# A gated mix of linear and local attention on one core: first loads in another order, and the range-test branch ahead of the last outputs

## The chip, the cores and the metric

The kernel runs on one core of one Trainium2 chip. The metric is the device time of one execution in microseconds. Three runs of the kernel before took 500.43, 500.95 and 501.45 us; the median is 500.95 us.

## What is computed

Two attention blocks A and B read the same tokens `x` (2048 tokens of 1024 features, bf16); a sigmoid gate per token mixes their outputs. Cut to what matters:

```python
x = A_x
g = sigmoid((x * gate_w).sum(-1, keepdims=True))
# A: linear attention, 32 heads of 32
q, k, v = split(x @ A_wqkv)
phi = lambda t: where(t > 0, t + 1, exp(t)) + 1e-6
kv, z = einsum("bhsd,bhse->bhde", phi(k), v), einsum("bhsd->bhd", phi(k))
o = einsum("bhqd,bhde->bhqe", phi(q), kv) / (einsum("bhqd,bhd->bhq", phi(q), z)[..., None] + 1e-6)
a = merge_heads(o) @ A_wo
# B: each token attends to 8 tokens, 2 apart, at and before its own
q, k, v = split(x @ B_wqkv)
attn = softmax(where(idx >= 0, q . k[idx] * scale, -1e9))    # idx = s - 2 * (0..7)
b = merge_heads(attn . v[idx]) @ B_wo
return g * a + (1 - g) * b
```

## The kernel before

**A program written as a list, ordered by a planner.** The function `plan` lists operations with `P.op` (engine, instruction, estimated cost, what is read and written, a priority). `Prog.schedule` (L120) plays the list through with those estimates, taking on each engine the ready operation of lowest priority number, and so fixes each engine's order. `move` (L1337) leaves it to the planner whether ScalarE (ACT) or VectorE (DVE) empties a PSUM bank. The planner makes six passes and keeps the shortest plan. `Prog.emit` (L202) then writes each engine's stream: the waits of an operation, the operation, its semaphore. Nothing is decided at run time but one branch, told of below. So an engine that waits holds up all that stands behind it in its stream, DMA issues included; SP's stream is nearly nothing but DMA issues.

**Stages on TensorE (PE).** First nine matmuls on zeros (L1348). Then B's values: 16 tiles of 128 tokens by two halves of 512 columns, each a group of eight 128x128x512 matmuls (L1309), copied from PSUM to `vst` (eight buffers, L1340 on DVE, L1341 on ACT) and stored to `vB_hbm` by SP (L1376). Then B's keys and queries by 512 tokens, with local attention of finished tokens (L1416, L1435, L1442) fitted between; A's keys, values and their sums (L1517); the fold of those sums into `A_wo` (L1569); A's queries, denominators (L1596) and outputs; last, B's output projection for each token tile (`final`, L1634 to 1656): eight matmuls into each of two banks, one DVE operation that mixes a bank with A's part into the output buffer `o` (two buffers, L1649), and one DMA of the tile by SP (L1655). The last tile is done in three parts of 512, 256 and 256 columns, each with a DMA of its own.

**The first loads.** Matmuls want `x` with features on partitions, so `xT` is loaded with transposing DMAs from SP. The first 512 tokens come as four transposes of 256 features each (L1297), the other tiles as one transpose for each 128 tokens (`load_x`, L1285). ScalarE issues the first half of B's value weight in four quarters (L1296), and, after a wait for a matmul, its second half in two loads (L1365). TensorE runs the first four tiles together, quarter by quarter (L1360 to 1364). The tiles go in the order 0 to 7 with the first weight half, 0 to 7 with the second, then 8 to 11 and 12 to 15 in the same way (L1353). Tiles 8 to 15, `gate_w` and the loads of `xn` (the tokens once more, for the gate, L1387) may not be issued before tile 5's first group (`x_op`, L1372). `early` (L1351) names the groups after which later weights are loaded.

**The range test.** Parts of the fast path hold only for inputs in some range. Maxima are collected on the way; after the third output tile of `final` a last chain of small DVE operations makes one number, `flag` (L1696), 1 for inputs in range. `tail` (L1718) ends each engine's stream: wait for `flag`, load it into a register (L1721); on SP, wait for every DMA semaphore of the program (39 of them, L1723); then a branch (L1725), in whose arm, for flag 0, stands a general path for any input (`progs`, hundreds of instructions on an engine). With these inputs the flag is 1 and the branch jumps over that arm.

Of the kernel before, what the change touches and what calls it, by code (L numbers as in the profile page):

```python
# [13 lines left out]
D = 1024  # L14
# [6 lines left out]
SCALE = DH ** -0.5  # L21
SZ = {BF16: 2, F32: 4, I32: 4}
# [39 lines left out]
class Prog:  # L62
# [139 lines left out]
    def emit(self, block, tail):  # L202
# [35 lines left out]
        def run(e, eng):  # L238
            for o, waits in plan[eng]:
                for s, v in waits:  # L240
                    e.wait_ge(s, v)
                ins = o.fn(e)
                ins.then_inc(o.val[0], 16 if o.chan is not None else 1)
            tail(e, eng)

        self.final = [(self.csem[c], n) for c, n in chan_n.items()]
        self.counts = cnt
# [855 lines left out]
def build_kernel(nc, A_x, A_wqkv, A_wo, B_x, B_wqkv, B_wo, gate_w, out):  # L1103
# [117 lines left out]
    def plan(seen):  # L1221
# [63 lines left out]
        def load_x(t, prio, after=()):  # L1285
            e_, r = t // 8, t % 8
            return P.op("sp", lambda e: e.dma_start_transpose(xT[:, :, t * 128:(t + 1) * 128], x2[e_, r * 128:(r + 1) * 128, :]),  # L1287
                        1.5, writes=[xT.part((0, 8), (t * 128, (t + 1) * 128))], prio=prio, chan="x%d" % t, lat=1.15, after=after)

        def load_w(slot, half, src, c0, prio, d0=0, d1=8, eng="sp", after=()):  # L1290
            n = d1 - d0
            return P.op(eng, lambda e: e.dma_start(ws[slot][:, d0:d1, half * 512:half * 512 + 512], src[:, d0:d1, c0:c0 + 512]), 0.4 + 0.2 * n,
                        writes=[ws[slot].part((d0, d1), (half * 512, half * 512 + 512))], prio=prio, chan="w%d_%d_%d" % (slot, half, d0), lat=0.42 * n, after=after)

        for d in range(0, 8, 2):
            load_w(0, 0, Bw, 2048, 0.1 + 0.1 * d, d, d + 2, "act")  # L1296
            P.op("sp", lambda e, d=d: e.dma_start_transpose(xT[:, d:d + 2, 0:512], x2[0, 0:512, 128 * d:128 * d + 256]),  # L1297
                 1.3, writes=[xT.part((d, d + 2), (0, 512))], prio=d / 2, chan="xd%d" % d, lat=1.2)
        for t in range(4, 8):
            load_x(t, 4 + t)  # L1300
# [50 lines left out]
        early = {(1, 1): (1, 0, Bw, 1024, 21), (4, 1): (2, 0, Bw, 0, 22), (7, 1): (1, 1, Bw, 1536, 23), (10, 1): (2, 1, Bw, 512, 24),  # L1351
                 (12, 1): (3, 0, Aw, 1024, 25), (14, 1): (3, 1, Aw, 1536, 26)}
        for t, half in [(t, half) for t0, n in ((0, 8), (8, 4), (12, 4)) for half in range(2) for t in range(t0, t0 + n)]:  # L1353
            vt, vs = vst.next()
            xs, xr = x_tile(t)
            w, wr = w_half(0, half)
            if t < 4 and half == 0:
                if t == 0:
                    first = [main.next() for _ in range(4)]
                    for d in range(0, 8, 2):  # L1360
                        for t_ in range(4):
                            if d == 6 and t_ == 0:
                                o_w = o
                            o = group(first[t_], x_tile(t_)[0], w, [xT.part((d, d + 2), (t_ * 128, t_ * 128 + 128)), ws[0].part((d, d + 2), (0, 512))], d, d + 2)
                    for d in range(0, 8, 4):  # L1365
                        load_w(0, 1, Bw, 2560, 3 + 0.1 * d, d, d + 4, "act", after=[o_w])
                bank = first[t]
            else:
                bank = main.next()
                o = group(bank, xs, w, [xr, ws[0].part((0, 8), (half * 512, half * 512 + 512))])  # L1370
                if (t, half) == (5, 0):
                    x_op = o  # L1372
                    for t_ in range(8, NT):
                        load_x(t_, 4 + t_, [o])
# [5 lines left out]
        P.op("sp", lambda e: e.dma_start(gwb[:, :], gate_w[None, :].to_broadcast([128, D])), 0.6, writes=[gwb.all()], prio=29, chan="gw", lat=0.8, after=[x_op])  # L1380
# [4 lines left out]
        for t in range(NT):  # L1385
            xt, xs_ = xn.next()
            P.op("sp", lambda e, t=t, xt=xt: e.dma_start(xt[:, :], x2[t // 8, (t % 8) * 128:(t % 8) * 128 + 128, :]), 0.6, writes=[xt.all()], chan="xn%d" % xs_, lat=1.0, after=[x_op])  # L1387
# [246 lines left out]
        def final(t):  # L1634
# [4 lines left out]
            for f0, f1 in parts:  # L1639
# [13 lines left out]
                if t == NT - 1 or f1 == 1024:  # L1653
                    c = f0 if t == NT - 1 else 0
                    P.op("sp", lambda e, e_=e_, r=r, o_=o_, c=c, f1=f1: e.dma_start(out2[e_, r * 128:(r + 1) * 128, c:f1], o_[:, c:f1]), 0.5,  # L1655
                         reads=[o_.part((c, f1))], chan="out%d_%d" % (os_, c), lat=1.0)
# [61 lines left out]
    def tail(e, eng):  # L1718
        reg = e.alloc_register("fast_ok")
        e.wait_ge(*flag_op.val)  # L1720
        e.reg_load(reg, flag[0:1, 0:1])  # L1721
        if eng == "sp":
            for s, v in P.final:  # L1723
                e.wait_ge(s, v)
        with e.If_eq(reg, 0):  # L1725
            for s, v in P.final + [(P.esem[x], n) for x, n in P.counts.items() if n]:
                e.wait_ge(s, v)
            for th in progs[eng]:
                th(e)

    with nc.Block() as block:
        P.emit(block, tail)
# [34 lines left out]
```

## Time and profile before

| what | value | how to read it |
|---|---|---|
| median of three runs | 500.95 us | the time that a change is measured against |
| the profiled execution | 500.95 us | its own time |
| span of that execution | 499.1 us | from its first instruction to its last |
| ACT busy | 165.8 us (33%) | one of the two engines that empty PSUM |
| L1309, values and other groups | 748 and 921 matmuls, 167.5 and 210.4 us | projections, by the order of their operands |
| L1645 | 259 matmuls, 55.3 us | B's output projection |
| DMA queue of SP (q1) | 48834 packets, 45.89 MB | nearly all transfers |
| DMA queue of ACT (q10) | 2144 packets, 2.10 MB | six weight loads at the start |

The page cuts the span into 40 slices of 12.5 us; in the row of the DMA engines a digit is the busy share of a slice in tenths, 9 for 90% and more:

```profile
PE   8899999999999999999999999999999999999995
DVE  2221336997577777556554645596865734524442
DMA  9999993331003037201100100501574315101122
```

In a line of a timeline stand the start, the length, the engine, the line of code, the operation and what it writes and reads, and in brackets how long the engine was idle before it and what ended that. A q behind an engine's name marks its sequencer, which loads registers, branches and issues DMAs.

### The profile page before, as it was taken

The page shows a single profiled execution, that of the slowest core. Times are in us where ns is not written, and L with a number is a line of the kernel's source. Part 1 is how long each engine was busy: PE and PEld are TensorE (multiplying, and loading weights), DVE is VectorE, ACT ScalarE, POOL GpSimd, SP SyncE. Part 2 cuts the span into 40 slices and gives each one's busy share as a digit, 9 for nine tenths or more (in the row PEclk, how much of TensorE's full clock was granted, in tenths as well). Part 3 has the DMA queues.
Part 4 walks back from the last instruction along what each step waited for, and adds up shares of the span by engine and source line. Part 5 has one row for each costly group of instructions (what it writes and reads, how often), then busy time and mean ns, then how long its engine had stood idle before and what let it go on. Part 6 is the DMA issues. An engine that isn't in the chain of part 4 may idle for free.

```text
span 499.1 us, 11394 instructions
## 1 busy us (share of the span) xinstructions
PE 480.8 (96%) x5055; PEld 227.4 (46%) x5121; DVE 276.7 (55%) x489; ACT 165.8 (33%) x285; POOL 5.1 (1%) x27
## 2 busy tenths in 40 slices
PE   8899999999999999999999999999999999999995
PEld 2344444444444444554554454444444444444442
DVE  2221336997577777556554645596865734524442
ACT  1111111123333445565655556355423322020000
POOL 3000000000000000000000000000000000000000
PEclk9999999999999999999999999999999999999999
DMA  9999993331003037201100100501574315101122
GB/s 193 206 204 301 324 353 104 105 107 42 2 24 106 24 80 206 56 24 41 29 22 25 35 12 4 168 2 35 159 188 101 90 24 165 62 4 66 65 84 68
DMA packets 51035, 48.80 MB, mean 98 GB/s; under 512 B 20129, under 2 KB 38945, under 8 KB 50978
## 3 DMA queue, kind: packets, MB, share of 16 engines
q1 hardware_dynamic: 48834, 45.89, 32.8%
q10 hardware_dynamic: 2144, 2.10, 1.9%
q8 instruction: 42, 0.69, 0.5%
q14 instruction: 15, 0.12, 0.1%
HBM read 34.34 MB, written 9.44 MB: 88 GB/s over the span
## 4 chain that ended last, share of the span: by engine, by line
PE 88%; DMA 4%; SPq 3%; DVE 2%; issue 2%; ACT 0%; ACTq 0%
PE ps_all L1309 70%; PE ps_all L1645 11%; PE ps_all L1416 2%; PE ps_all L1435 2%; DMA xT<-in_A_x_dram 2%; SPq L1297 2%; DMA rb<-rc_hbm 1%; PE ps_all L1517 1%; SPq L1609 1%; SPq L1287 1%; DMA rc_hbm<-ra 1%; PE ps_all L1442 1%; DVE zsel L1559 1%; DVE pq L1322 0%; PE ps_all L1596 0%
## 5 line engine op out<-in xcount | busy, mean ns | idle before, releaser
L1309 PE MATMUL ps_all<-w,xT 128*128 128x512 bf16 x921 | 210.4, 384 | 8.1 <-issue 4.3
L1309 PE MATMUL ps_all<-xT,w 128*128 128x512 bf16 x748 | 167.5, 379 | 2.3 <-issue 1.9
L1309 PEld LDWEIGHTS ps_all<-w,xT 128*128 128x128 bf16 x960 | 92.1, 99 | 114.6 <-issue 9.2
L1309 PEld LDWEIGHTS ps_all<-xT,w 128*128 128x128 bf16 x768 | 73.8, 98 | 89.1 <-issue 1.8
L1645 PE MATMUL ps_all<-w,qT 128*128 128x512 bf16 (+1 forms) x259 | 55.3, 372 | 0.3
L1645 PEld LDWEIGHTS ps_all<-w,qT 128*128 128x128 bf16 x264 | 25.9, 98 | 29.6
L1340 DVE CAST vst<-ps_all 128x512 bf16<-128x512 f32 x17 | 11.6, 691 | 48.5 <-PE ps_all L1309 48.5
L1320 DVE TENSOR_SCALAR e<-e 128x512 bf16<-128x512 bf16 x64 | 18.3, 290 | 34.4 <-ACT e L1318 17.2
L1422 ACT ACTIVATE E<-ps_all 128x1824 bf16<-128x1824 f32 (+1 forms) x18 | 30.4, 1688 | 10.2 <-PE ps_all L1416 9.5
L1318 ACT ACTIVATE e<-ps_all 128x512 bf16<-128x512 f32 x32 | 19.1, 597 | 42.8 <-PE ps_all L1309 42.3
L1425 DVE TENSOR_TENSOR E<-E,msk 128x1824 bf16<-128x1824 bf16 (+1 forms) x18 | 19.8, 1102 | 22.4 <-ACT E L1422 22.4
L1649 DVE SCALAR_TENSOR_TENSOR o<-ps_all,gm,xT 128x512 bf16<-128x512 f32 (+1 forms) x25 | 18.2, 730 | 22.9 <-PE ps_all L1645 22.8
L1316 ACT ACTIVATE e<-ps_all 128x512 bf16<-128x512 f32 x32 | 19.1, 597 | 26.6 <-PE ps_all L1309 25.8
L1341 ACT ACTIVATE vst<-ps_all 128x512 bf16<-128x512 f32 x15 | 9.0, 597 | 53.3 <-PE ps_all L1309 53.3
L1454 DVE TENSOR_TENSOR qT<-ps_all,L 128x456 bf16<-128x456 f32 (+1 forms) x36 | 21.0, 627 | 6.2 <-ACT L L1452 5.0
L1274 DVE TENSOR_TENSOR mx<-mx,kT 128x1024 bf16<-128x1024 bf16 x32 | 20.8, 688 | 3.0 <-ACT kT L1341 2.8
L1322 DVE SCALAR_TENSOR_TENSOR pk<-ps_all,e 128x512 bf16<-128x512 f32 x32 | 21.9, 688 | 0.7
L1451 ACT ACTIVATE L<-ps_all 128x456 f32<-128x456 f32 (+1 forms) x36 | 17.8, 547 | 12.4 <-PE ps_all L1435 12.4
L1274 DVE TENSOR_TENSOR mx<-mx,qT 128x1024 bf16<-128x1024 bf16 x32 | 20.7, 688 | 1.4 <-ACT qT L1344 1.2
L1341 ACT ACTIVATE kT<-ps_all 128x512 bf16<-128x512 f32 x16 | 9.6, 597 | 34.2 <-PE ps_all L1309 34.2
L1344 ACT ACTIVATE qT<-ps_all 128x512 bf16<-128x512 f32 x16 | 9.6, 597 | 33.1 <-PE ps_all L1309 33.1
L1612 DVE TENSOR_TENSOR xT<-xT,rb 128x512 bf16<-128x512 bf16 x24 | 16.3, 688 | 6.8 <-DMA rb<-rc_hbm 6.3
(72 smaller groups left out, 284.9 us busy)
## 6 DMA issues: line engine op xcount, KB each, us to landing
rb<-rc_hbm SPq DMA_DIRECT2D x32, 256.0 KB, 4.8
w<-in_A_wqkv_dram SPq DMA_DIRECT2D x6, 1024.0 KB, 7.7
v<-vB_hbm SPq DMA_DIRECT2D x36, 128.0 KB, 2.7
vB_hbm<-vst SPq DMA_DIRECT2D x32, 128.0 KB, 5.0
w<-in_B_wqkv_dram SPq DMA_DIRECT2D x4, 1024.0 KB, 6.3
xn<-in_A_x_dram SPq DMA_DIRECT2D x16, 256.0 KB, 2.6
out_dram<-o SPq DMA_DIRECT2D x15, 256.0 KB, 2.0
w<-in_A_wo_dram SPq DMA_DIRECT2D x8, 256.0 KB, 3.6
```

The source lines that it names most:

```text
L1274: P.op("dve", lambda e, m=m, op=op: e.tensor_tensor(m[:, 0:n], m[:, 0:n], src, op), 0.08 + n / 1920.0, reads=[m.all(), reg], writes=[m.all()],
L1309: last = e.matmul(bank.ap(), lhs(dc), rhs(dc), start=(dc == 0), stop=(dc == 7))
L1316: P.op("act", lambda e: e.activation(e_[:, :], bank.ap(), ACT.Exp), act(512), reads=[bank.iv], writes=[e_.all()])
L1318: P.op("act", lambda e: e.activation(e_[:, :], bank.ap(), ACT.Exp, accum_out=qe[:, col:col + 1]), act(512) + 0.1, reads=[bank.iv], writes= ...
L1320: P.op("dve", lambda e: e.tensor_scalar(e_[:, :], e_[:, :], 1.0, 1e-6, op0=ALU.min, op1=ALU.add), 0.25, reads=[e_.all()], writes=[e_.all()])
L1322: P.op("dve", lambda e: e.scalar_tensor_tensor(out=dst, in0=bank.ap(), scalar=0.0, in1=e_[:, :], op0=ALU.max, op1=ALU.add), dps(512), read ...
L1341: fa = lambda e: e.activation(dst, src(), ACT.Copy)
L1422: P.op("act", lambda e: e.activation(E[:, 0:32 * nq].rearrange("p (j q) -> p j q", j=4), ps[:, 4:8, 0:8 * nq], ACT.Exp), act(32 * nq), rea ...
L1425: P.op("dve", lambda e: e.tensor_tensor(ev(), ev(), m[:, :, :].rearrange("p r q -> p (r q)")[:, None, :].to_broadcast([128, 16, 2 * nq]), ...
L1454: P.op("dve", lambda e, L=L, h=h, q0=q0: e.tensor_tensor(qT[:, :, q0:q0 + nq], SO[h].ap(0, n).rearrange("p (c q) -> p c q", c=8), L[:, 0:n ...
L1645: last = e.matmul(bank.ap(0, f1 - f0), qT[:, dc, t * 128:(t + 1) * 128], ws[3][:, dc, f0:f1], start=(dc == 0), stop=(dc == 7))
L1649: P.op("dve", lambda e, bank=bank, o_=o_, t=t, n=n, i0=i0, i1=i1, tgt=tgt, c0=c0: e.scalar_tensor_tensor(out=o_[:, i0 * 128:i1 * 128].rear ...
```

## The change

Two parts of the program change.

At the start, the four transposes of 512 tokens go; every tile is loaded by `load_x`. The first weight half is loaded in four quarters, two from ScalarE and two from SP behind tile 0; the second half in four quarters from SP behind tile 3 (each `load_w` of two feature blocks). The tiles are worked through in blocks of four, each with the first and then the second half; tile 0's groups wait quarter by quarter. The gates on later loads go, and `early`'s first entry is moved from group (1, 1) to (2, 0). Two latency estimates of the planner are changed.

At the end, an engine's stream is cut before the operations that the planner starts in its last microseconds (`BACK`: 19 for SP, 14 for DVE, 30 for ACT, none for the others), and not before the flag. The cut-off rest is written into both arms of the branch. In the new order of instructions the arms hold seven output DMAs on SP, nine mixing operations on DVE, and the program's last output DMA, columns 768 to 1024 of the last tile, on ScalarE. In the arm for inputs in range SP waits at its end only for the semaphores of DMAs that nothing else waited for, four of them, and the arm ends with a jump of its own.

```diff
+BACK = {"sp": 19, "dve": 14, "act": 30}
...
-    def emit(self, block, tail):
+    def awaited(self, chan):
+
+        return all(o.users for o in self.ops if o.chan == chan)
+
+    def emit(self, block, tail, flag_op):
...
-        def run(e, eng):
-            for o, waits in plan[eng]:
+        def go(e, ops):
+            for o, waits in ops:
                 for s, v in waits:
                     e.wait_ge(s, v)
                 ins = o.fn(e)
                 ins.then_inc(o.val[0], 16 if o.chan is not None else 1)
-            tail(e, eng)
+
+        def run(e, eng):
+            ops = plan[eng]
+            k = len(ops)
+            while k and ops[k - 1][0].start > max(self.span - BACK.get(eng, 0), flag_op.end + 3):
+                k -= 1
+            go(e, ops[:k])
+            tail(e, eng, lambda: go(e, ops[k:]))
 
         self.final = [(self.csem[c], n) for c, n in chan_n.items()]
+        self.last = [(self.csem[c], n) for c, n in chan_n.items() if not self.awaited(c)]
...
-        def load_x(t, prio, after=()):
+        def load_x(t, prio):
...
-                        1.5, writes=[...], prio=prio, chan="x%d" % t, lat=1.15, after=after)
+                        1.5, writes=[...], prio=prio, chan="x%d" % t, lat=1.3)
...
-        for d in range(0, 8, 2):
-            load_w(0, 0, Bw, 2048, 0.1 + 0.1 * d, d, d + 2, "act")
-            P.op("sp", lambda e, d=d: e.dma_start_transpose(xT[:, d:d + 2, 0:512], x2[0, 0:512, 128 * d:128 * d + 256]),
-                 1.3, writes=[xT.part((d, d + 2), (0, 512))], prio=d / 2, chan="xd%d" % d, lat=1.2)
-        for t in range(4, 8):
-            load_x(t, 4 + t)
+        load_x(0, 0)
+        load_w(0, 0, Bw, 2048, 0.1, 0, 2, "act")
+        load_w(0, 0, Bw, 2048, 0.2, 2, 4, "act")
+        load_w(0, 0, Bw, 2048, 0.3, 4, 6)
+        load_w(0, 0, Bw, 2048, 0.4, 6, 8)
+        for t in range(1, NT):
+            load_x(t, 3 + t)
+        for d in range(0, 8, 2):
+            load_w(0, 1, Bw, 2560, 6.1 + 0.1 * d, d, d + 2)
+        P.op("sp", lambda e: e.dma_start(gwb[:, :], gate_w[None, :].to_broadcast([128, D])), 0.6, writes=[gwb.all()], prio=29, chan="gw", lat=0.8)
...
-        early = {(1, 1): (1, 0, Bw, 1024, 21), ...
+        early = {(2, 0): (1, 0, Bw, 1024, 21), ...
-        for t, half in [(t, half) for t0, n in ((0, 8), (8, 4), (12, 4)) for half in range(2) for t in range(t0, t0 + n)]:
+        for t, half in [(4 * b + i, half) for b in range(NT // 4) for half in range(2) for i in range(4)]:
             vt, vs = vst.next()
             xs, xr = x_tile(t)
+            bank = main.next()
             w, wr = w_half(0, half)
-            if t < 4 and half == 0:
-                if t == 0:
-                    first = [main.next() for _ in range(4)]
-                    for d in range(0, 8, 2):
-                        for t_ in range(4):
...
-                            o = group(first[t_], x_tile(t_)[0], w, [...], d, d + 2)
-                    for d in range(0, 8, 4):
-                        load_w(0, 1, Bw, 2560, 3 + 0.1 * d, d, d + 4, "act", after=[o_w])
-                bank = first[t]
-            else:
-                bank = main.next()
-                o = group(bank, xs, w, [...])
-                if (t, half) == (5, 0):
-                    x_op = o
-                    for t_ in range(8, NT):
-                        load_x(t_, 4 + t_, [o])
+            step = 2 if t == 0 else 8
+            for d in range(0, 8, step):
+                o = group(bank, xs, w, [xr, ws[0].part((d, d + step), (half * 512, half * 512 + 512))], d, d + step)
...
-                    P.op("sp", lambda e, ...: e.dma_start(out2[...], o_[:, c:f1]), 0.5,
+                    P.op("act" if f1 == 1024 and c else "sp", lambda e, ...: e.dma_start(out2[...], o_[:, c:f1]), 0.5,
...
-    def tail(e, eng):
+    def tail(e, eng, rest):
         reg = e.alloc_register("fast_ok")
         e.wait_ge(*flag_op.val)
         e.reg_load(reg, flag[0:1, 0:1])
-        if eng == "sp":
-            for s, v in P.final:
-                e.wait_ge(s, v)
         with e.If_eq(reg, 0):
+            rest()
             for s, v in P.final + [(P.esem[x], n) for x, n in P.counts.items() if n]:
                 e.wait_ge(s, v)
             for th in progs[eng]:
                 th(e)
+        with e.Else():
+            rest()
+            if eng == "sp":
+                for s, v in P.last:
+                    e.wait_ge(s, v)
```

## The prediction

> **What bounds the kernel now.** The profile's first page, for the engine that fills the span:
>
> ```profile
> span 499.1 us, 11394 instructions
> PE 480.8 (96%) x5055; PEld 227.4 (46%) x5121; DVE 276.7 (55%) x489; ACT 165.8 (33%) x285; POOL 5.1 (1%) x27
> ```
>
> TensorE is the bound nearly everywhere, so a gain must come from the 18.3 us in which it is not busy. The view of waits, TensorE's alone, says where those are:
>
> ```profile
> PE ps_all L1309 <- issue: 6.2, 39, 0.2
> PE ps_all L1309 <- DMA xT<-in_A_x_dram: 3.2, 2, 2.2
> PE ps_all L1348 <- DVE warm L1266: 1.3, 1, 1.3
> PE ps_all L1596 <- DVE xT L1322: 0.3, 1, 0.3
> ```
>
> The 6.2 us are 39 switches of matmul shape, which nothing here touches. The one wait on work is 3.2 us for transposed tokens. The timeline of TensorE puts it at the start, and the table of stretches, for line 1309 alone (length, PE busy and count, weight loads, granted clock, DMA share, GB/s), shows what follows it:
>
> ```profile
> 6.25 14.20 PE L1309 MATMUL ps_all<-w,xT 128*128 128x512 bf16 x55 [0.98 <-DMA xT<-in_A_x_dram]
> 22.63 37.67 PE L1309 MATMUL ps_all<-w,xT 128*128 128x512 bf16 x163 [2.19 <-DMA xT<-in_A_x_dram]
> ```
>
> ```profile
> 0.00:6.25 6.25, 0.00 (x0) 0.03 (x1) 1.00 0.78 175
> 6.25:10.23 3.98, 3.98 (x10) 1.39 (x11) 1.00 1.25 227
> 10.23:20.45 10.22, 10.16 (x47) 4.41 (x45) 1.00 1.09 168
> 20.45:23.88 3.43, 1.25 (x6) 0.61 (x7) 1.00 1.14 341
> 23.88:27.30 3.42, 3.42 (x9) 1.22 (x8) 0.50 1.19 224
> ```
>
> After the wait of 2.19 us the clock is granted at 0.50 for 3.42 us. There and up to 10.23 a matmul takes 3.42/8 = 0.427 us; at full clock eight take 1.73 us (DVE's outputs start at 486.32 and 488.05), 0.216 each. The wait is the first one for tile 7, whose transpose was issued at 13.21 and landed 9.3 us later, beside the second half of the weight, issued by ScalarE at 13.57.
>
> The other place is behind the last matmul, 493.2 to 499.1. By line, the flag's load (L1721), the 39 closing waits (L1724), the branch (L1725) and the drains (L1731):
>
> ```profile
> L1721 DVEq TENSOR_LOAD <-flag x1: 542/542/542, 493.3 to 493.3; - x1
> L1721 SPq TENSOR_LOAD <-flag x1: 504/504/504, 494.7 to 494.7; - x1
> L1724 SPq EVENT_SEMAPHORE  x39: 27/28/28, 495.3 to 498.0; - x39
> L1725 PEldq COMPARE_BRANCH  x1: 3764/3764/3764, 491.4 to 491.4; - x1
> L1725 SPq COMPARE_BRANCH  x1: 58/58/58, 498.1 to 498.1; - x1
> L1731 DVEq DRAIN  x1: 59/59/59, 497.0 to 497.0; - x1
> L1731 SPq DRAIN  x1: 57/57/57, 498.9 to 498.9; - x1
> ```
>
> The trace has the last output issued at 494.25 and landed at 496.71. SP steps through waits long fulfilled until 498.06, some 0.07 us each, and only then branches: 1.35 us after the last byte.
>
> **The start.** Removed: four transposes of 512 tokens by 256 features, the wait before ScalarE's two half-weight loads, and the gates on x tiles 8 to 15, gate_w and xn. Added, in SP's order: tile 0 whole, two quarters of the first weight half (the other two stay on ScalarE), tiles 1 to 3, four quarters of the second half, the first store, tiles 4 and 5. TensorE now does four tiles by both halves, so 64 matmuls need 4 tiles (1.05 MB) and the weight (2.10 MB), where before the first 64 needed 8 tiles and half a weight: the same bytes.
>
> I count to 69.8 matmuls, which before were done at 27.30: 56 by 20.45, 1.25/0.216 = 5.8 by 23.88, 8 at half clock. After: tile 0 is issued at 0.80 like the first transpose, which landed 5.3 us later; a first matmul at 6.25 again. Eight at 0.427 to 9.66, 1.3 more to 10.23, then full clock: 60.5 x 0.216 = 13.1, done at 23.3. That is 4.0 us earlier if nothing stalls. Does it? Bytes moved before, from the table: 1.09 MB by 6.25, 1.99 by 10.23, then 0.168 MB a us. Tile 1 completes 1.57 MB, at 8.4 (wanted 9.66); tile 2 1.84 MB at 9.6 (wanted 11.7); tile 3 2.10 MB at 10.9 (wanted 13.4). The last weight quarter completes 3.15 MB, at 17.1; wanted at 16.4: a stall of 0.7. The stall of 0.5 us at 9.44 did not keep the clock from rising, so I charge 0.7 alone: **3.3 us gained**. SP's issues fit: a transpose 1.31 each, a quarter some 0.5, in all 4 x 1.31 + 6 x 0.5 = 8.2 us from 0.80; if they are held as the third one was (2.92), tile 3 is issued by 9.08 as the fourth was, and the quarters by 11.2, still 4 us ahead of their need. The first store then waits for ScalarE's eviction near 10.5, with tiles 4 and 5 behind it: issued by 14, landing 4.5 later at 18.5 and, tile after tile, 1.6 apart; TensorE wants them from 22.7 on, 1.73 apart.
>
> Bounds: at best tile 0 lands 3.0 us after issue (the shortest transpose) and TensorE runs on from its warm-up at 5.27: 5.0 gained. At worst tile 0 takes 7.2 us (the longest of the first four): 1.8 late, with one more window at half clock (1.7) and the 0.7: -0.2.
>
> The Trainium skill (TensorE: Matmul & The Clock Gate, Part 1) has the array go cold after a window of about 3.4 us that is idle. Here one idle for 2.2 of its 3.4 us was enough, so the row decides. By the page the stall cost no clock and this part would be worth 1.7 less, 1.6.
>
> Later order: the planner moves DVE's xn products back and swaps which engine evicts a few banks. Costed at nothing, since from 27.3 on TensorE waits for no eviction there; four banks of 1.73 us are the cover, and an xn product that came in front uncovered would cost its 1.22 us.
>
> **The tail.** The flag (437.0) is long ready, so no arm waits for it. In the new order SP branches with seven outputs left, DVE with nine results, ScalarE with one DMA, PE and POOL with nothing. ACT took 2.4 us from branch to drain (448.9 to 451.3), POOL 2.6, DVE 3.1, PE 3.8, SP 0.7. DVE: its result at 479.41 ends 480.16; load 0.54, branch 0.07, jump 3.1: back at 483.9, where the next was due at 481.14, 2.8 late. Each later result has 0.98 us of idle time ahead of it, so three regain it; the two output buffers are free (2.0 us to landing), and TensorE has eight banks. SP: output of 473.29, then 0.50 + 0.06 + up to 3.8: back by 478.0, due 476.74; DVE wants that buffer at 481.14. Both at nothing; the cover is 9 x 0.98 = 8.8 us for DVE, and beyond it every us counts.
>
> The Trainium skill (Runtime: NRT & Kernel Launch, Instruction fetch mechanics) speaks against this: a taken branch out of the fetched pages waits for a fetch. The jumps of 2.4 to 3.8 us agree; it gives no length. Taken alone it would charge DVE's 2.8 us to the end, 498.9; the rows of idle time before each result say that it is absorbed.
>
> At the end, DVE's last result stands at 493.73. ScalarE can issue at 493.76 where SP issued at 494.25, held by the issue before it (1.32 us). At SP's 2.46 to landing it lands at 496.22, but the output before landed at 496.53 (3.6), so that one decides. Four waits remain, passed on landing; then branch, drain and barrier as before, 499.1 - 498.06 = 1.04: 496.6 + 1.0 = 497.6, **1.5 us gained**. The long queue of 39 waits goes; PE's drain at 495.26 is next. Bounds: the added branch at an arm's end free, and the earlier landing: 496.22 + 0.3, 2.5 gained; ScalarE's idle queue as slow as 3.6 with one more 0.7 jump: 0.6 gained or, at two jumps, nothing.
>
> **Sum.** 500.95 (this execution's time, also the median; span 499.1 and 1.85 around it) - 3.3 - 1.5 = 496.1.
>
> **Rivals.** *The start gives nothing*: the lower bound above, -0.2. For it: one transpose did take 7.2 us. Against: it was the second, not the first. 500.95 + 0.2 - 1.5 = 499.6.
>
> *Tiles crawl behind copies, slower*: mechanism in one place, SP's single queue, where transposes now follow weight quarters. If each tile lands 3.28 us after its forerunner, as the second did (9.40 after 6.12), tile 1 (two quarters at 1.0 between) is there at 11.4, tile 3 at 18.0, the weight at 22. TensorE is idle half the time, stays at half clock until 24.9, and reaches 69.8 matmuls near 31.3, 4.0 later than before: 500.95 + 4.0 - 1.5 = 503.4. Against: the later tiles came 0.9 to 1.6 apart. It turns slower by 1.0 us (0.2%) where the start loses 2.5, at a pitch near 2.9.
>
> *The jump surfaces*: DVE's takes more than the 8.8 us can cover. No row is near; at 10 us DVE would be 10 + 0.6 - 8.8 = 1.8 late at the end, 497.9.
>
> *Only the tail works and the start loses about 1.5*: 501.0, no change.
>
> **Chances.** The forecast 0.75 (own range 493.5 to 498.7: both best bounds, 5.0 and 2.5; at worst one more half-clock window, 3.3 - 1.7, and 0.6). Start gives nothing 0.10, surfaced jump 0.01, no change 0.07, crawl 0.07. What the measurement can tell is 0.2%, 1.0 us: faster 0.86, same 0.07, slower 0.07. The range 493.6 to 499.6 leaves out the last two, half of the second case and a little below.
>
> **What would show it.** Right: no wait for xT over 1 us after 10 us, no clock of 0.50 after 10.3, TensorE past its first 64 matmuls by 23; DVE late near the branch and on time four results later; four closing waits, under 1.3 us from last landing to end. Wrong: a half-clock window between 10 and 30, tiles over 2 us apart, DVE's last result later than 0.6 us after the last matmul, or new waits of TensorE for evictions between 60 and 125.

## The result and the profile after

The changed kernel takes 492.72 us (median of six runs, 491.94 to 494.49) where the kernel before, run beside it, takes 499.9 (498.04 to 501.45): a ratio of 0.9864, interval 0.9833 to 0.9894. The forecast of 496.1 had the direction and both places of the gain, but both were larger: the time lies 0.9 us below its range. About 1.05 us of the distance is not the change's: the forecast set out from 500.95, and the kernel before took 499.9 beside the changed one. The profiled execution after took 494.49 us, with a span of 492.6; it is set here against the profiled execution before (500.95, span 499.1).

The first page of the profile after, and under it TensorE's waits (line, what ended the wait, us in total, times, longest):

```profile
span 492.6 us, 11357 instructions
PE 478.7 (97%) x5055; PEld 226.9 (46%) x5121; DVE 274.4 (56%) x487; ACT 166.9 (34%) x287; POOL 5.0 (1%) x27
```

```profile
PE ps_all L1326 <- issue: 6.0, 38, 0.2
PE ps_all L1365 <- DVE warm L1279: 1.2, 1, 1.2
PE ps_all L1326 <- DMA xT<-in_A_x_dram: 1.2, 1, 1.2
PE ps_all L1598 <- DVE xT L1339: 0.7, 1, 0.7
```

Of 3.2 us of waits for transposed tokens 1.2 are left, the one before the first matmul on tokens. TensorE's timeline and the table of stretches for line 1326, the old 1309 (length, PE busy and count, weight loads, granted clock, DMA share, GB/s), show that nothing follows it:

```profile
6.47 33.71 PE L1326 MATMUL ps_all<-w,xT 128*128 128x512 bf16 x144 [1.20 <-DMA xT<-in_A_x_dram]
```

```profile
6.47:10.16 3.69, 3.69 (x9) 1.34 (x10) 1.00 1.15 228
10.16:20.45 10.29, 10.24 (x48) 4.68 (x48) 1.00 1.00 229
20.45:23.88 3.43, 3.43 (x18) 1.54 (x17) 1.00 0.86 169
23.88:27.30 3.42, 3.42 (x18) 1.53 (x17) 1.00 1.18 181
```

Half clock still holds up to 10.16: the matmuls start 0.43 us apart there and 0.216 apart behind it. (The clock column prints 1.00 in the first row because the profile's first entry for the clock is the one at 10.16.) Behind 10.16 there is no stall and no second stretch at 0.50. The last two rows have 18 matmuls each, against 6 and 9 before.

The end, by line: the flag's load (L1723), the branch (L1724), the closing waits (L1734), the jump at the arm's end (L1730), the drains (L1736).

```profile
L1724 SPq COMPARE_BRANCH  x1: 57/57/57, 470.5 to 470.5; - x1
L1724 DVEq COMPARE_BRANCH  x1: 72/72/72, 476.3 to 476.3; - x1
L1724 PEldq COMPARE_BRANCH  x1: 3704/3704/3704, 487.8 to 487.8; - x1
L1734 SPq EVENT_SEMAPHORE  x2: 17/22/28, 492.1 to 492.1; - x2
L1730 SPq COMPARE_BRANCH  x1: 43/43/43, 492.2 to 492.2; - x1
L1736 DVEq DRAIN  x1: 524/524/524, 489.6 to 489.6; - x1
L1736 SPq DRAIN  x1: 13/13/13, 492.4 to 492.4; - x1
```

SP and DVE branch some 22 and 16 us before the end, and SP's last step after the last byte (492.06) is short. One instruction holds up to two waits, so four semaphores are two wait instructions and the jump, which carries the fourth; the 39 instructions before held two each as well and the branch behind them one more, 79 semaphores in all and not 39 as the description of the kernel before has it.

**Where the 6.5 us came from.** The middle of the program is the same: from the first matmul of B's keys to the end of the last matmul of all it is 425.73 us before and 425.98 after, and 425.1 to 426.1 in every profile of this study. So each profile is told by two numbers: when the key matmuls begin, and how long after the last matmul the span ends.

| profile | keys begin | last matmul to end | clock first full | later at half clock |
|---|---|---|---|---|
| before | 67.48 | 5.93 | 10.23 | 23.88 to 27.30 |
| after | 63.54 | 3.10 | 10.16 | none |

The start gives 3.94, the middle takes 0.25 back (TensorE's wait for the denominators at L1598 is 0.7 us instead of 0.3), the tail gives 2.83, in all 6.5.

### The profile page after: what moved, and what is told of

The parts are those of the page before. It is cut to its first block, busy times and chain, and to the rows that moved or that the text cites. A ratio compares the mean times of both kernels' runs of the same rounds, so it can differ in the third digit from the quotient of the medians.

```text
span 492.6 us, 11357 instructions
## 1 busy us (share of the span) xinstructions
PE 478.7 (97%) x5055; PEld 226.9 (46%) x5121; DVE 274.4 (56%) x487; ACT 166.9 (34%) x287; POOL 5.0 (1%) x27
## 4 chain that ended last, share of the span: by engine, by line
PE 91%; DMA 3%; DVE 2%; issue 2%; SPq 1%; ACT 1%; ACTq 0%
PE ps_all L1326 74%; PE ps_all L1647 11%; PE ps_all L1418 2%; PE ps_all L1437 2%; DMA rb<-rc_hbm 1%; DMA xT<-in_A_x_dram 1%; PE ps_all L1519 1%; SPq L1611 1%; PE ps_all L1444 1%; DMA rc_hbm<-ra 1%; DVE zsel L1561 1%; DVE pq L1339 0%; PE ps_all L1598 0%; PE ps_all L1571 0%; DVE e L1337 0%
## 5 line engine op out<-in xcount | busy, mean ns | idle before, releaser
L1357 DVE CAST vst<-ps_all 128x512 bf16<-128x512 f32 x15 | 10.4, 692 | 45.7 <-PE ps_all L1326 45.7
L1358 ACT ACTIVATE vst<-ps_all 128x512 bf16<-128x512 f32 x17 | 10.1, 597 | 49.4 <-PE ps_all L1326 49.4
```

The costliest lines, as they stand in the source:

```text
L1358: fa = lambda e: e.activation(dst, src(), ACT.Copy)
```

## The experiments

Two theories stood at the outset. Mine: the start and the tail each bring what the trace shows, the start by the transposes that no longer come late. Its rivals: one edit brings all; and within the tail, it is the shorter list of waits, or the other queue for the last output, and not the branch's place.

**The change once more.** The same kernel, for a second profile.

> The changed kernel once more, beside the others. If the gain is 4.0 us at the start and 2.8 us behind the last matmul (the difference of the two traces: TensorE 3.9 ahead at the end of the value stage, 3.7 at the last matmul; last result to end 5.4 and 2.6 us), it is 6.0 to 7.5 us faster than the kernel before. If the granted clock explains the spread of both (a free-running window that catches or misses the stall), this run's profile shows full clock from a time between 6.8 and 10.3 us on and nothing else that differs; rival: the spread lies in the tail, and the time from the last matmul to the end differs by over 1 us from the 3.1 of the first profile.

491.81 us (491.56 to 493.63), ratio 0.9858 (0.9828 to 0.9889). By the medians that is 8.5 us below the kernel before, more than the 6.0 to 7.5 expected. The clock is full from 4.56 on, earlier than expected, where the first profile had it from 10.16; the loads land earlier too, tile 0 at 5.60 instead of 6.42. The keys begin at 61.74, 1.80 earlier. The tail is 2.80. TensorE's timeline:

```profile
5.65 2.20 PE L1326 MATMUL ps_all<-w,xT 128*128 128x512 bf16 x8 [0.66 <-DMA xT<-in_A_x_dram]
8.05 32.27 PE L1326 MATMUL ps_all<-w,xT 128*128 128x512 bf16 x145 [0.20 <-DMA xT<-in_A_x_dram]
```

The shares of clock and loads can be estimated from the first profile: at full clock its first eight matmuls would have ended at 8.20 and the ninth started when tile 1 landed, at 8.64, so that the tenth, which started at 10.23, comes at 8.86. That makes 1.4 us for the clock and 0.4 for the loads.

**The start alone, and the tail alone.** The first takes the tail of the kernel before into the changed kernel, the second its start.

```diff
# start alone
     def tail(e, eng, rest):
+        rest()
         reg = e.alloc_register("fast_ok")
         e.wait_ge(*flag_op.val)
         e.reg_load(reg, flag[0:1, 0:1])
+        if eng == "sp":
+            for s, v in P.final:
+                e.wait_ge(s, v)
...
# tail alone
+        for d in range(0, 8, 2):
+            load_w(0, 0, Bw, 2048, 0.1 + 0.1 * d, d, d + 2, "act")
+            P.op("sp", lambda e, d=d: e.dma_start_transpose(xT[:, d:d + 2, 0:512], ...
...
+        for t, half in [(t, half) for t0, n in ((0, 8), (8, 4), (12, 4)) for half in range(2) for t in range(t0, t0 + n)]:
```

> The new start and tile order with the old tail. Theory (the start gives 3.7 to 4.0, half of it stall and half clock): 3.2 to 4.2 us faster than before, no wait for xT after 7 us, no window at half clock after 10.3. Rival (the start gives what the forecast gave it at worst, and the rest came with the branch): 0 to 2 us faster.

> The old start with the new tail. Theory: 2.5 to 3.0 us faster than before, under 2.8 us from the last result to the end, and the stall of about 2.2 us for tile 7 stays with its half-clock window. Rival (the tail is worth the 1.5 of the forecast and the start more): 1.2 to 1.8 us faster. Rival (DVE's branch surfaces): not faster than 0.5 us, the last result over 1 us after the last matmul's end.

Start alone: 495.3 us, ratio 0.9915 (0.989 to 0.994); keys at 61.90, tail 5.69. Tail alone: 498.13, ratio 0.9962 (0.9943 to 0.998); keys at 67.60, tail 3.07. Each edit moves its own number and leaves the other's, and the two ratios multiply to 0.988, beside 0.986 for both. That one edit brings all has fallen. The sizes were missed a little: by the medians the start alone is 5.0 us faster (3.2 to 4.2 expected), the tail alone 2.2 (2.5 to 3.0 expected).

**Why the transposes were late.** In the kernel before, the transposes that TensorE waits for run beside weight loads of ScalarE's queue: the second one beside the four quarters, tile 7 beside the second half. The kernel before with the second half moved to SP's queue, behind the tiles:

```diff
-                        load_w(0, 1, Bw, 2560, 3 + 0.1 * d, d, d + 4, "act", after=[o_w])
+                        load_w(0, 1, Bw, 2560, 11.1 + 0.1 * d, d, d + 4)
```

> The kernel before with one edit: the second half of the value weight is issued by SP behind tile 7 and without a wait, not by ScalarE beside it. Theory (tile 7 was late because that megabyte moved beside it): tile 7 lands by 18.5 us, the wait of 2.2 us falls below 0.5 and no window at half clock follows: 3 to 4 us faster. Rival (transposes come at a pace of their own, and eight tiles are too many for the first 22 us): the wait stays over 1.5 us, no faster than 1 us. Third: the half weight becomes the late one, a wait of 1 to 3 us for it at 22 us in place of the other, within 1 us of before.

498.56 us, ratio 0.9967 (0.9945 to 0.9989). TensorE's timeline of it:

```profile
5.66 1.90 PE L1309 MATMUL ps_all<-w,xT 128*128 128x512 bf16 x8 [0.81 <-DMA xT<-in_A_x_dram]
10.07 30.13 PE L1309 MATMUL ps_all<-w,xT 128*128 128x512 bf16 x129 [2.51 <-DMA xT<-in_A_x_dram]
```

The wait for tile 7 is gone: it landed at 17.79, where before it landed at 22.50. The wait for the second transpose is there, now 2.51 us, and the clock went to 0.50 from 11.12 to 14.53. Half of the cause was taken away, and part of the gain came: keys at 65.30, and 1.8 us by the medians where 3 to 4 were expected.

The same from the other side, the changed kernel with all four quarters on ScalarE's queue:

```diff
-        load_w(0, 0, Bw, 2048, 0.3, 4, 6)
-        load_w(0, 0, Bw, 2048, 0.4, 6, 8)
+        load_w(0, 0, Bw, 2048, 0.3, 4, 6, "act")
+        load_w(0, 0, Bw, 2048, 0.4, 6, 8, "act")
```

> The changed kernel with all four quarters of the first weight half issued by ScalarE, as the kernel before did it, and tile 1 directly behind tile 0 on SP. Theory (weight from a second queue beside the first two transposes makes the second transpose late: 9.4 to 10.0 us with four quarters beside it, 8.0 to 8.6 with two): tile 1 lands at 9.4 to 10.0 us, a wait of 1 to 2.5 us for it where the clock is full early, and where it is, a half-clock window behind it: 0.8 to 3 us slower than the changed kernel. Rival (the two queues only share the same bytes): tile 1 by 8.6, within 0.3 us of it.

```profile
6.04 1.04 PE L1326 MATMUL ps_all<-w,xT 128*128 128x512 bf16 x4 [0.77 <-DMA xT<-in_A_x_dram]
7.47 0.60 PE L1326 MATMUL ps_all<-w,xT 128*128 128x512 bf16 x2 [0.40 <-DMA w<-in_B_wqkv_dram]
9.40 30.82 PE L1326 MATMUL ps_all<-w,xT 128*128 128x512 bf16 x142 [1.32 <-DMA w<-in_B_wqkv_dram]
```

493.96 us, ratio 0.9877 (0.9855 to 0.9899), and in the timeline two waits that the changed kernel has not. The fourth quarter, issued at 2.29, landed at 9.35, and tile 1, issued at 2.23 beside it, at 9.55, after 7.3 us: the tile ends with the copies of the other queue. In the change, where two of the quarters and the tiles share SP's queue, tile 1 took 5.3 (3.34 to 8.64) and the last first-half quarter 4.9, so the same bytes (half the weight and two tiles) were there at 8.64, in its second profile at 8.00. Keys at 63.37, some 1.5 later than in the profiles of the change with an early clock. The traces show it; the interval overlaps that of the change (0.9858 and 0.9864), so the times do not settle it.

**Old tile order, new order of loads.** Three kernels go on from the kernel before and keep its tiles 0 to 7 by halves and its four transposes. In the first, two quarters and the second half go to SP's queue; in the second, the second half also stands ahead of the first stores (both have the old tail); the third is the second with the new tail.

```diff
-            load_w(0, 0, Bw, 2048, 0.1 + 0.1 * d, d, d + 2, "act")
+            load_w(0, 0, Bw, 2048, 0.1 + 0.1 * d if d < 4 else d / 2 - 0.5, d, d + 2, "act" if d < 4 else "sp")
...
-                        load_w(0, 1, Bw, 2560, 3 + 0.1 * d, d, d + 4, "act", after=[o_w])
# the first of the three
+                        load_w(0, 1, Bw, 2560, 11.1 + 0.1 * d, d, d + 4)
# the second and third, with load_x(t, 3 + 0.1 * t) for tiles 4 to 7
+                        load_w(0, 1, Bw, 2560, 3.8 + 0.01 * d, d, d + 4)
```

> The kernel before with two edits to its loads and none to its tile order, its transposes of 512 tokens or its tail: the last two quarters of the first weight half are issued by SP between those transposes, and the second half by SP behind tile 7. Theory (the loss of the old start is weight moving on a second queue beside transposes, whatever their form and the tile order): no wait for xT over 0.6 us after 6 us, first key matmul at 61.7 to 63.7 us as with the new start, 3.5 to 5 us faster than before. Rival (the tile order by fours or the transposes of one tile are part of the gain): first key matmul after 64.5 us, waits over 1 us stay, under 3 us faster.

> The run with both edits once more, with the second weight half issued by SP directly behind tile 7 and ahead of the first stores; in that run five stores stood between its two pieces and TensorE waited 2.8 us for the second. Theory (order of the loads on one queue is all; tile order and form of transposes do not matter): tile 7 by 16.5 us, the half by 20.5, no wait over 1 us after 6 us and no half-clock window, first key matmul at 61.7 to 64.0 us: 3.5 to 5.5 us faster than before, as the new start alone (0.9915). Rival (the order by fours is needed, since eight tiles and the whole weight are wanted sooner by it): a wait of 1.5 us or more stays at tile 7 or at the half, first key matmul after 65 us, under 2.5 us faster.

> The same loads and old tile order with the new tail. Theory: the two parts add up, 0.984 to 0.988 of before, the changed kernel's own ratio within its interval. Rival (as above): 0.990 or more.

The first: 499.23 us, ratio 0.9986 (0.9965 to 1.0008), no change where 3.5 to 5 us were expected. Its timeline:

```profile
5.49 14.45 PE L1309 MATMUL ps_all<-w,xT 128*128 128x512 bf16 x64 [0.22 <-DMA xT<-in_A_x_dram]
22.77 17.40 PE L1309 MATMUL ps_all<-w,xT 128*128 128x512 bf16 x72 [2.84 <-DMA w<-in_B_wqkv_dram]
```

The tokens are in time (the second transpose landed at 6.33, tile 7 at 16.22), so the cause of the late transposes is confirmed a second time; but a new wait took its place. The weight's last piece was issued at 17.32, behind five stores, and TensorE stood 2.84 us, with a stretch of half clock after it. The second kernel mends that: 496.37 us, ratio 0.9928 (0.9906 to 0.9949), keys at 64.09, a wait of 2.4 us for the weight, no half clock; by the medians 2.8 us faster where 3.5 to 5.5 were expected. The third: 494.0 us, ratio 0.9891 (0.9872 to 0.9909), keys at 63.61, tail 3.00:

```profile
5.64 5.34 PE L1322 MATMUL ps_all<-w,xT 128*128 128x512 bf16 x24 [0.37 <-DMA xT<-in_A_x_dram]
11.41 8.96 PE L1322 MATMUL ps_all<-w,xT 128*128 128x512 bf16 x40 [0.43 <-DMA xT<-in_A_x_dram]
22.16 18.09 PE L1322 MATMUL ps_all<-w,xT 128*128 128x512 bf16 x83 [1.79 <-DMA w<-in_B_wqkv_dram]
```

What is left is the tile order, and with it the form of the first transposes, which these kernels keep. The first 64 matmuls need the same bytes in either order, 3.15 MB; but in the old order the 65th wants the other half of the weight at once, 1.05 MB more, which landed at 22.1 in the third kernel, and in the new order it wants one tile, 0.26 MB. By the profiles the order of loads brings the keys from 67.5 to some 63.8 and the rest on to 61.8. By the times the second part is not settled: 0.9891 beside 0.9858, with intervals that overlap.

**The kernel before, two more looks.** To see how much the start of one kernel varies.

> The kernel before, one more profile, for the state of its clock. Theory (the old start waits for transposes whatever the clock does): first key matmul at 65.6 to 67.7 us, 1.7 less where no half-clock window follows the wait for tile 7; if the clock is full before 7 us, the wait for the second transpose is 1.8 to 2.6 us instead of 0.5. Rival: an early clock makes the old start faster by the same 1.7 us as the new one, first key matmul under 65.5 with the half-clock window.

> As the look before it, a second execution: same expectations.

501.2 us and 498.82 us. TensorE in the first of the two:

```profile
5.57 2.08 PE L1309 MATMUL ps_all<-w,xT 128*128 128x512 bf16 x8 [0.30 <-DMA xT<-in_A_x_dram]
9.98 10.53 PE L1309 MATMUL ps_all<-w,xT 128*128 128x512 bf16 x48 [2.34 <-DMA xT<-in_A_x_dram]
23.44 16.74 PE L1309 MATMUL ps_all<-w,xT 128*128 128x512 bf16 x70 [2.93 <-DMA xT<-in_A_x_dram]
```

Here the clock was full from 5.98 on, the first eight matmuls took 2.08 us, and it gained nothing: TensorE stood 2.34 us for the second transpose and 2.93 for tile 7. Keys at 68.08, 0.6 later than in the profile of before. The other look had one wait of 2.09 us, ending at 10.37, half clock from 10.67 to 14.08 and keys at 65.60. There the matmuls were so late that ScalarE issued its second half only at 15.72, 1.6 us behind tile 7's transpose, and tile 7 landed after 3.7 us instead of 9.3: the same finding without an edit. So an early clock with early loads is worth 1.8 us to the new start, which waits for next to nothing, and nothing sure to the old one.

**More warm-up.** Twelve matmuls on zeros in place of nine, to fill the gap before the first tile.

```diff
-    WARM = 9
+    WARM = 12
```

> The changed kernel with 12 instead of 9 matmuls on zeros ahead of the first load, so that TensorE is busy without a gap from 1.25 us until tile 0 lands at 5.6 to 6.4. Theory (the spread between runs is the clock's window: full clock from 4.6, 6.8 or 10.2 us, and a gap of 1.0 to 1.2 us keeps a window from counting, one of 0.6 does not): full clock no later than 8.1 us in every run, the slow end of the spread (493.6 to 494.5) is gone, median 0.3 to 1.2 us below the changed kernel's, that is 0.984 to 0.986 of before. Rival (the warm-up only delays the first matmul): 0.3 to 0.6 us slower than the changed kernel. No operation but the matmuls on zeros differs.

492.31 us, ratio 0.9856 (0.9832 to 0.9881): the change with nine gave 0.9858 and 0.9864. No difference shows. The clock was full from 4.18, keys at 61.94. One profile and five times (492.01 to 493.5) cannot tell whether the slow end of the spread is gone.

**The tail in parts.** Three kernels, each the change with one part of the tail undone: the branch behind everything (`BACK` empty, so an engine's arm holds nothing but SP's closing waits); all DMA semaphores waited for at the end of the arm; the last output DMA on SP's queue.

```diff
# branch last
-BACK = {"sp": 19, "dve": 14, "act": 30}
+BACK = {}
...
# all waits
-                for s, v in P.last:
+                for s, v in P.final:
...
# last output on SP
-                    P.op("act" if f1 == 1024 and c else "sp", lambda e, ...
+                    P.op("sp", lambda e, ...
```

> The changed kernel with nothing in the arms: every engine branches after its last operation; SP still waits for four semaphores and the last output stays on ScalarE. Theory (taking the branch early is worth what the slowest jump is late): DVE's jump of 3.1 to 5.9 us after its last result ends the span, 4.5 to 7.3 us behind the last matmul instead of 2.8 to 3.1: 1.5 to 4 us slower than the changed kernel. Rival (the gain of the tail lies in the waits and the queue alone): within 0.5 us of it.

> The changed kernel, but SP waits in its arm for all 39 semaphores as the kernel before did. Theory: SP begins them after its last issue and needs 39 x 0.07 = 2.8 us, of which the landing covers 1.6: 1.0 to 1.4 us slower than the changed kernel, 3.9 to 4.4 us from the last matmul to the end. Rival (the waits lie beside the landing): within 0.3 us.

> The changed kernel with the last output DMA back on SP. Theory: it is issued 0.4 us later, behind SP's issue of 1.28 us, and lands last: 0.4 to 0.9 us slower, 3.3 to 3.9 us from the last matmul to the end. Rival (the DMA before it lands last anyway, as the forecast had it): within 0.2 us.

| kernel | us | ratio (interval) | last matmul to end |
|---|---|---|---|
| change | 492.72 and 491.81 | 0.9864 (0.9833 to 0.9894), 0.9858 (0.9828 to 0.9889) | 3.10, 2.80 |
| branch last | 495.47 | 0.9904 (0.9875 to 0.9934) | 5.32 |
| all waits | 493.63 | 0.9868 (0.9837 to 0.99) | 3.95 |
| last output on SP | 492.6 | 0.986 (0.9833 to 0.9887) | 3.23 |

The branch's place carries the tail: 2.2 to 2.5 us of it by the traces. The intervals of branch last and of the change still touch, but its four times (494.11 to 495.75) lie above all four of last output on SP, run beside it (492.23 to 493.52). With the branch last, SP's instructions stand so:

```profile
L1724 SPq COMPARE_BRANCH  x1: 58/58/58, 489.8 to 489.8; - x1
L1734 SPq EVENT_SEMAPHORE  x2: 17/22/28, 492.8 to 492.9; - x2
L1736 SPq DRAIN  x1: 13/13/13, 493.1 to 493.1; - x1
```

The branch itself is 58 ns, and SP's next instruction comes 3.0 us later. The last byte was there at 491.28, so this jump ends the program, and not DVE's as was expected: DVE's drain stands at 491.57, ScalarE's at 492.60, SP's at 493.10. In the change SP branches at 470.55 and issues its next output at 473.16, 19 us before the end. The full list of waits costs 0.85 to 1.15 us of tail; SP is through it 1.05 us behind the last byte (489.94):

```profile
L1734 SPq EVENT_SEMAPHORE  x40: 27/28/28, 488.6 to 491.0; - x40
L1730 SPq COMPARE_BRANCH  x1: 43/43/43, 491.1 to 491.1; - x1
```

That is 0.061 us a step. It shows in the trace and not in the times, whose intervals overlap. The other queue for the last output shows in neither: 0.1 to 0.4 by the traces, no more than the two profiles of the change differ.

## Why the prediction was wrong in its sizes, and what it had right

The forecast was wrong by two terms of its sum. The start, put at 3.3 us, gave 3.94 in the profiled pair and 5.1 in the mean of all profiles: the sum charged half clock up to 10.23 ("Eight at 0.427 to 9.66, 1.3 more to 10.23, then full clock"), which six of seven profiles of the new start did not have, and a stall of 0.7 that did not come. The tail, put at 1.5, gave 2.83: "branch, drain and barrier as before", 1.04, measured 0.56, and the last byte, put 2.80 us behind DVE's last result, came after 2.02. The mechanism at both places was right.

**The bound and both places: right.** No wait for `xT` over 1 us came after 10 us, and no clock of 0.50 between 10.3 and the end; TensorE was past 64 matmuls near 22.0 (10.16 and 55 more at 0.216). SP's issues fitted: tiles 1 to 3 landed at 8.64, 9.63 and 10.75, where 8.4, 9.6 and 10.9 had been worked out from bytes. The rival in which tiles crawl behind copies at a pitch near 3.3 is refuted by the same three numbers. Its mechanism is real, but it sat in the kernel before, between two queues, and the change took it away. Tiles 6 to 8 did land 2.0 to 4.2 us apart (17.83, 19.86, 22.34, 26.52), which the prediction had named as a sign of being wrong; TensorE waited for none of them.

**The start: one term mis-sized, and a frame too narrow.** The sum had 4.0 us gained, less a stall of 0.7 for the last weight quarter, "17.1; wanted at 16.4". The quarter landed at 15.51 and no stall came: the table has 228 and 229 GB/s up to 20.45, where the forecast went on from 10.23 at the 0.168 MB a us of the old order. So the profiled pair gained 3.94, 0.6 over the term.

The larger part is in what the forecast never varied. It charged the new start with half clock up to 10.23 because the one execution of the kernel before that it knew had that. In seven profiles with the new start (the change twice, start alone, the warm-up and the three of the tail) the keys begin at 63.54 once and at 61.6 to 62.1 six times; in four with the old start they begin at 65.6 to 68.1, 67.2 in the mean. The mean of the seven is 62.1, a gain of 67.2 - 62.1 = 5.1, not 3.3; the ratio of start alone, 0.9915, makes it 4.2. When the clock rises differs from execution to execution in both kernels: in the six it was full between 4.18 and 6.72 us, and tile 0 landed at 5.60 to 5.84. Of the two starts only the new one showed a gain from an early rise. The best bound of 5.0 is near this by luck: it was worked out from a landing of tile 0 at 3.8, not from the clock.

**The clock, row and rule.** The forecast went by the row: a stand of 2.19 us of a 3.42 us stretch cost a stretch at half clock. More profiles narrow this. The clock's entries at 0.50 last 3.41 us, those at full clock between them 3.41, 6.83, 13.65 and 17.07, whole multiples of it. Counted in stretches of 3.41 us from the moment of full clock, one in which TensorE stood 2.09 us or more (six cases, up to 2.84) was followed by half clock; 1.87, 1.79 and 1.74 were not, nor was a wait of 2.43 us that fell 1.5 and 0.9 into two stretches. The Trainium skill (TensorE: Matmul & The Clock Gate, Part 1) has the clock fall after an idle window of about 3.4 us. The window's length agrees with the rows; that all of it must be idle does not, and the measurements decide.

**The tail: too small by 1.3 us, from two terms.** From the last matmul to the end it was 5.93 us before and 3.10 after. In parts:

| part | before | forecast | after |
|---|---|---|---|
| last matmul to DVE's last result | 0.52 | 0.52 | 0.52 |
| to the last byte | 2.98 | 2.80 | 2.02 |
| to the end of the span | 2.42 | 1.1 | 0.56 |

The third row's error is the added jump at the end of the arm, which the forecast charged like the old one ("branch and barrier as before", 1.04 us). Behind the old branch, which goes over the whole general path, SP's drain followed by 0.8 us (498.1 to 498.9); behind the new one it follows by 0.17 (492.22 to 492.39). Why the new jump is short was not tested; that its target lies near is likely. The bound "free" was close, the value taken was not.

The second row's error has a likely cause that the forecast did not see. It took the 3.6 us from issue to landing of the output before the last over from the kernel before. After, that output is still the one that decides, but it took 2.9 us (489.20 to 492.06). In the kernel before, the last of the sixteen parts of each of the last two outputs landed 0.73 and 1.04 us after the fifteenth, and while they moved, code was loaded (the queues of kind instruction). The transfers of the last microseconds (queue, kind: packets, MB, share), in the kernel before from 490 to 499:

```profile
q1 hardware_dynamic: 576, 0.52, 17.7%
q8 instruction: 2, 0.03, 1.6%
q14 instruction: 3, 0.02, 0.9%
```

and after, from 486 to 493, with no row for q14:

```profile
q1 hardware_dynamic: 538, 0.64, 26.2%
q10 hardware_dynamic: 144, 0.07, 3.3%
q8 instruction: 2, 0.03, 2.0%
```

In the kernel before one of the three begins 1.0 us after DVE's branch (493.83, 494.87). All sixteen profiles sort by it: in the eight with a branch behind the last results, such a load begins between DVE's last result and the last byte, which comes 2.5 to 3.0 us after the result; in the eight with the early branch none begins there, and it comes after 1.8 to 2.2. "Branch last" is among the first eight although its last output is on ScalarE's queue (2.74), "last output on SP" among the second (2.21). So the early branch seems also to take code loading out of the way of the last outputs. The profiles with the early branch hold a second sign of it: beside the load of q8, which stands 1.2 us behind TensorE's branch (488.91 and 487.75 after), the output issued at 488.59 had its last part 0.97 us after its fifteenth, and 0.89 to 1.22 in all eight. That is a regular coincidence in sixteen profiles and not a proof: the output issued at 489.20 ran beside the same load and had no late part, and no kernel varies the load alone.

**The jumps' cover: right, with less to spare.** DVE's jump was put at 3.1 us, 2.8 late, made good within three results. In the timeline of DVE after (start, length, line, in brackets the idle time and its end):

```profile
475.73 0.75 DVE L1651 SCALAR_TENSOR_TENSOR o<-ps_all,gm,xT 128x512 bf16<-128x512 f32 x1 [0.97 <-PE ps_all L1647]
482.20 2.73 DVE L1651 SCALAR_TENSOR_TENSOR o<-ps_all,gm,xT 128x512 bf16<-128x512 f32 x4 [5.72 <-issue]
485.77 1.41 DVE L1651 SCALAR_TENSOR_TENSOR o<-ps_all,gm,xT 128x512 bf16<-128x512 f32 x2 [0.85 <-DMA out_dram<-o]
487.81 1.36 DVE L1651 SCALAR_TENSOR_TENSOR o<-ps_all,gm,xT 128x512 bf16<-128x512 f32 x2 [0.63 <-PE ps_all L1647]
489.56 0.48 DVE L1651 SCALAR_TENSOR_TENSOR o<-ps_all,gm,xT 128x256 bf16<-128x256 f32 x1 [0.39 <-PE ps_all L1647]
```

It branched at 476.32, and its next result began at 482.20 where one was due near 477.45: 4.7 late. The jump itself was as forecast, 3.3 us to DVE's next instruction (a wait, 479.62); the sum had no term for the 2.6 us that follow it, for outputs that had landed by 479.54. Five of the eight profiles with the early branch have this second stand (5.4 to 5.9 us from the branch to the next result); old tile order with new tail, quarters on ScalarE and tail alone do not, and there the result came after 3.2 to 3.3, 2.1 to 2.2 late. Behind the branch the five have three code loads on q14 and these three have two; why was not tested. In the profile shown, that result and five more run with no wait for TensorE, one of them after 0.85 us for an output buffer, which the forecast had held free; at 487.81, with three results left, DVE waits for TensorE again. Of the cover of 8.8 us over half was used. The rival of the surfaced jump did not come, but its distance was 4 us, not 6.

**Sum.** For the profiled pair: the start 0.6 too little, less 0.25 lost in the middle, and the tail 1.3 too little make, within rounding, the 1.6 us by which 496.1 misses 494.49. The median of 492.72 is another 1.8 lower. The second profile, with a time of 491.66, has the early clock; the runs between were not profiled, so that the clock explains them too is likely and not shown. That the start gives nothing, and that only the tail works, are refuted by start alone (0.9915, interval 0.989 to 0.994).

## What to carry to other kernels

A profile shows one course of the clock at the start: ask what each kernel would do with another, for here the start that waited for next to nothing gained from an early clock, and the one that waited for loads did not. Put transposing loads and the copies that they need beside them into one queue in the order of need, and let a block of work ask for its next bytes in small pieces, so that no single transfer stands between two groups; by the times of these kernels that last step is not settled. Take a branch that must be taken where the engine still has idle time ahead of its remaining work: here 22 us before the end on SP and 16 on DVE hid the jumps, and other distances were not tried. The closing waits can be those that nothing else has waited for.

## What the runs showed of the hardware that was not expected

- A transposing load ended late when plain loads of another queue ran beside it: 7.2 to 8.1 us from issue to landing for the second transpose beside ScalarE's four quarters, 4.1 to 4.6 with the last two quarters behind it in SP's own queue; 8.8 to 9.8 us for tile 7 beside the second half, 3.5 to 4.2 without.
- The clock rose after a stretch of 3.41 us in which TensorE stood 0.56 us or less, and did not after 0.82, 0.98 and 1.20. Where the stretches begin differs from execution to execution: full clock was first seen between 4.18 and 10.23 us.
- From a branch to the next instruction it took SP 0.17 us at the end of an arm, 0.5 to 0.8 over the general path and 2.6 to 3.0 into an arm; TensorE's branch took 3.6 to 3.9; DVE's next instruction came after 2.9 to 3.3, and where it had results left, the next one after 3.2 to 3.3 in three profiles and 5.4 to 5.9 in five.
- With a code load beginning between DVE's last result and the last byte, that byte came 2.85 us after the result in the mean of eight profiles; without one, 1.97 in the mean of eight.
